# Scores of a split-precision attention: three products passed head by head, or product by product over a PSUM bank

## The chip, the cores and the metric

The kernel runs on one core of a Trainium2 chip. The metric is the device time of one execution in microseconds (us). The kernel before took 839.26 us, the median of three runs (838.55 to 841.31).

## What is computed

Three layers follow one another. The first is a linear attention with a complex decay for each of 4 batches, 8 heads, 768 positions and 48 channels of a head:

```python
new_re = ar * S_re - ai * S_im
new_im = ar * S_im + ai * S_re
kv = np.einsum('bhd,bhe->bhde', k[:, :, t], v[:, :, t])
S_re, S_im = (new_re + kv, new_im)
y[:, :, t] = np.einsum('bhd,bhde->bhe', q[:, :, t], S_re)
```

The second mixes tokens (`relu(xt @ w_tok1) @ w_tok2`, 256 wide) and channels (`relu(u @ w_ch1) @ w_ch2`, 1536 wide), each with a residual. The third mixes each token with the one before it, and gives `sigmoid(xr @ w_r) * (relu(xk @ w_k)**2 @ w_v)`.

## The kernel before, in words

The recurrence is done in chunks. A sequence of 768 positions is six chunks of 128, here called rounds 0 to 5 (`J` in the code). Within a round the scores of the 128 keys against the 128 queries are formed for each head, masked to the lower triangle, and multiplied by v; what came before the round arrives through a carried state. Every fp16 operand is a pair, a high part (`h`) and a low part (`l`), and a product of two such pairs is three matmuls that add up in PSUM: high by high, high by low and low by high. `THREE` in `attention` (line 326) lists them.

One round runs through short stages, each a function of `attention`:
- `s_b`, `s_c` (lines 523 and 547) scale q and k and turn them by the angle (`Wc`, line 549, on VectorE), and ScalarE rounds them to the high parts `qh`, `kh` (line 550).
- `s_e` (line 559) forms the low parts `ql`, `kl` on VectorE (line 562).
- `transposed` (line 519) sends each of the four through a transposing DMA on SyncE's queue into `Rc` (for odd rounds of batch 0 the k parts go to `kt`). In batch 0 the order on the queue is qh, kh, ql, kl, in the others qh, ql, kh, kl.
- `s_f` (line 568), for a group g of four heads, forms the scores of the four heads in one PSUM bank, the tile `sp`: 128 columns a head, 12 matmuls in all (each 96 rows deep, 128 columns). `MM` (line 464) issues them, so the trace shows them under line 464.
- `s_m` (line 606) masks the bank (`m`, line 608, VectorE) and rounds it (line 609, ScalarE); `s_g` (line 612) forms its low part (line 613, VectorE).
- `s_h` (line 616) forms the output `y` of the round by matmuls from q and the carried state, and from the masked scores and v; `s_u`, `s_v` (lines 580, 597) carry the state on. `s_i` (line 631) evacuates `y` to the halves `xh` and `xl`.

In batch 0 the two groups have a bank each (two buffers); in the later batches both use one bank in turn. The order in which the stages of neighbouring rounds are written stands in `ORD0` (batch 0) and `ORD1`:

```python
ORD0 = "u1 f01 f11 b0 q0 k0 e0 i2 v1 m01 m11 g01 g11 h01 h11 w0"
```

The digit at the end says how many rounds back the stage works. Within that, the framework orders the instructions of each engine when the program is built: it keeps a list by priority and planned time, takes what its plan holds ready, and keeps the instructions that write one bank in the order written. On the chip every engine then follows its list in order, whatever is ready.

Batch 0's attention runs alone, from about 50 to 121 us into the span. In its first three rounds, and in its chunk sums, matmuls that compute nothing (`keep_busy`, line 466, `h1b<-tri`) stand behind the real ones at the lowest priority. From 121 us on the dense layers of batch b (`mm3`, line 681) run with the attention of batch b+1 mixed between them, up to about 690 us; the rest is the dense work of batch 3.

Of the kernel before, what the change touches and what calls it, by code (L numbers as in the profile page):

```python
# [98 lines left out]
def split_path(  # L99
# [224 lines left out]
    def attention(b):  # L324

        THREE = (("h", "h"), ("h", "l"), ("l", "h"))
# [136 lines left out]
        def MM(**k):  # L463
            last_mm[:] = [nc.tensor.matmul(**k)]  # L464
# [103 lines left out]
        def s_f(J, g):  # L568
            d = st[J]
            sp = (ps_d if b == 0 else ps_1).tile([128, 4, 128], F32, tag="d" if b == 0 else "s", name="sp")  # L570
            with tc.high_priority(offset=P_PE):
                for i in range(4):
                    h = 4 * g + i
                    for n_, (a_, b_) in enumerate(THREE):
                        MM(out=sp[:, i], lhsT=Tr[J % 2]["k" + a_][0:96, h], rhs=Tr[J % 2]["q" + b_][0:96, h],
                                         start=n_ == 0, stop=n_ == 2)
            d["S", g] = sp
            return 0.0

# [71 lines left out]
        cq, ck = late(s_c, "q"), late(s_c, "k")  # L651
        fns = {"b": s_b, "w": s_w, "q": cq, "k": ck, "e": s_e, "i": s_i, "u": s_u, "v": s_v}
        fns.update({nm + str(g): late(fn, g) for nm, fn in (("f", s_f), ("g", s_g), ("h", s_h), ("m", s_m)) for g in range(2)})
        order = [(fns[x[:-1]], int(x[-1])) for x in (ORD0 if b == 0 else ORD1).split()]

# [527 lines left out]
```

## Time and profile before

| | |
|---|---|
| median of 3 runs | 839.26 us |
| span of the profiled execution, first to last instruction | 832.8 us |
| between the two | 6.5 us |
| TensorE matmuls (PE) busy | 747.2 us, 6287 instructions |
| VectorE (DVE) busy | 589.9 us |
| ScalarE (ACT) busy | 521.0 us |
| score matmuls (`sp`) | 576 |

The time of the profiled execution itself is not given apart from its span; the row below it sets the span against the median of the runs. PE is TensorE's matmul row, PEld its weight loads, DVE VectorE, ACT ScalarE, SPq SyncE's queue. A matmul's row includes its way through the array, so that rows overlap: how fast a run of matmuls goes is read from the time between starts. "[1.88 <-DMA Rc<-kl]" behind a row says that the engine sat idle for 1.88 us ahead of it, until the DMA from `kl` to `Rc` landed.

### The profile page before, as it was taken

The numbers are of one execution on the slowest core, as the hardware profiler recorded it, in microseconds if no ns is written. First come the engines' busy times: TensorE is split into PE (matmuls) and PEld (weight loads), VectorE is DVE, ScalarE is ACT, GpSimd is POOL, SyncE is SP. The second block draws the span as 40 slices with busy tenths as digits, with TensorE's granted clock in tenths as the row PEclk, the third lists the DMA queues.
The fourth block names the chain that finished last, engine by engine and source line by source line (L and its number), as shares of the span: only waits on it lengthen the run. The fifth ranks groups of instructions, "written<-read, shape, count | busy, mean of one in ns | idle before, by whom it ended". The sixth has DMA issues, their size and how long they took to land.

```text
span 832.8 us, 15537 instructions
## 1 busy us (share of the span) xinstructions
PE 747.2 (90%) x6287; PEld 471.7 (57%) x6287; DVE 589.9 (71%) x1028; ACT 521.0 (63%) x993; POOL 21.0 (3%) x53
## 2 busy tenths in 40 slices
PE   0977768999889789999998989999999999999996
PEld 0666645446455555665665655566665666665553
DVE  4988789999989776886857647777776534584822
ACT  7775488667659579663748787566756533142742
POOL 3000000000000000000000000000000000010000
PEclk9999979999999899999999999999999999999998
DMA  7357973356762950161525521141604432867300
GB/s 230 114 119 158 204 195 116 124 176 160 165 180 57 205 133 30 40 122 49 86 36 111 113 76 39 39 109 19 119 11 87 80 105 52 274 204 251 112 29 33
DMA packets 137950, 94.94 MB, mean 114 GB/s; under 512 B 104592, under 2 KB 120208, under 8 KB 137872
## 3 DMA queue, kind: packets, MB, share of 16 engines
q1 hardware_dynamic: 137872, 93.88, 45.0%
q8 instruction: 51, 0.84, 0.4%
q14 instruction: 27, 0.22, 0.1%
HBM read 63.97 MB, written 4.72 MB: 82 GB/s over the span
## 4 chain that ended last, share of the span: by engine, by line
PE 47%; DVE 19%; ACT 17%; DMA 12%; issue 3%; SPq 0%; ACTq 0%; DVEq 0%
PE ps L681 21%; PE a L681 14%; PE y L464 4%; DMA Rc<-kl 4%; PE sp L464 3%; ACT X L331 3%; PE u L464 2%; DVE g L774 2%; DMA X<-by_time_a_re_dram 2%; ACT tmp L812 2%; DMA Rc<-ql 2%; DVE tmp L813 1%; DVE Wc L549 1%; DMA CH<-in_qk_dram 1%; DVE wf L265 1%
## 5 line engine op out<-in xcount | busy, mean ns | idle before, releaser
L681 PEld LDWEIGHTS <-wc 128*128 128x128 f16 x1728 | 166.2, 98 | 117.2 <-issue 10.5
L681 PE MATMUL a<-g,wc 128*128 128x384 f16 x864 | 160.5, 326 | 0.0
L681 PE MATMUL ps<-uh,wc 128*128 128x384 f16 x576 | 156.1, 326 | 2.9 <-DVE g L774 1.4
L464 PEld LDWEIGHTS <-Rc 96*128 96x128 f16 (+1 forms) x1488 | 84.4, 100 | 57.8 <-DMA Rc<-kh 10.7
L681 PE MATMUL a<-wv,g 128*128 128x384 f16 x576 | 111.5, 328 | 3.3 <-ACT g L847 3.3
L681 PE MATMUL ps<-xkh,wk 128*128 128x384 f16 x384 | 105.4, 327 | 1.9 <-DVE g L848 1.9
L773 ACT ACTIVATE g<-ps 128x384 f16<-128x384 f32 x96 | 46.4, 484 | 92.8 <-PE ps L681 92.7
L681 PE MATMUL ps<-ul,wc 128*128 128x384 f16 x288 | 93.8, 326 | 0.0
L774 DVE SCALAR_TENSOR_TENSOR g<-ps,g 128x384 f16<-128x384 f32 x96 | 53.0, 553 | 45.2 <-ACT g L773 45.0
L464 PE MATMUL sp<-Rc 96*128 96x128 f16 x504 | 61.4, 229 | 26.1 <-DMA Rc<-kh 8.5
L681 PEld LDWEIGHTS <-g 128*128 128x128 f16 x576 | 54.5, 98 | 38.2 <-ACT g L847 5.2
L681 PEld LDWEIGHTS <-wk 128*128 128x128 f16 x576 | 55.0, 98 | 36.0 <-issue 4.2
L464 PE MATMUL y<-CH,Rc 96*128 96x48 f16 (+1 forms) x984 | 69.5, 188 | 6.2 <-DMA Rc<-qh 2.2
L848 DVE TENSOR_TENSOR g<-ps,g 128x384 f16<-128x384 f32 x64 | 35.4, 553 | 41.7 <-ACT g L847 41.5
L681 PE MATMUL ps<-xkl,wk 128*128 128x384 f16 x192 | 62.9, 327 | 0.0
L845 ACT ACTIVATE ps<-ps 128x384 f32<-128x384 f32 x64 | 30.3, 473 | 37.9 <-PE ps L681 33.1
L608 DVE TENSOR_TENSOR m<-sp,tri 128x512 f32<-128x512 f32 x48 | 32.6, 685 | 23.1 <-PE sp L464 23.0
L549 DVE TENSOR_TENSOR Wc<-cs,X 128x768 f32<-128x768 f32 x48 | 44.9, 950 | 0.2
L464 PE MATMUL u<-CH,kh 128*128 128x48 f16 x320 | 39.2, 185 | 2.6 <-ACT kh L550 2.6
L331 ACT ACTIVATE X<-X,col_c 128x1152 f32<-128x1152 f32 x32 | 40.1, 1252 | 0.4 <-DVE X L374 0.2
L681 PE MATMUL ps<-wr,xrh 128*128 128x384 f16 x144 | 37.8, 330 | 0.8 <-DVE g L774 0.7
L609 ACT ACTIVATE Rc<-m 128x512 f16<-128x512 f32 x42 | 26.2, 623 | 19.1 <-DVE m L608 13.5
(215 smaller groups left out, 1391.9 us busy)
## 6 DMA issues: line engine op xcount, KB each, us to landing
wst<-in_moe_w_ch_dram SPq DMA_DIRECT2D x24, 768.0 KB, 4.4
CH<-in_qk_dram SPq DMA_DIRECT2D x24, 384.0 KB, 3.3
wst<-in_moe_w_tok_dram SPq DMA_DIRECT2D x8, 768.0 KB, 4.7
wst<-in_moe_w_k_dram SPq DMA_DIRECT2D x8, 768.0 KB, 4.7
wst<-in_moe_w_v_dram SPq DMA_DIRECT2D x8, 768.0 KB, 4.5
X<-by_time_a_re_dram SPq DMA_DIRECT2D x8, 576.0 KB, 4.6
X<-by_time_a_im_dram SPq DMA_DIRECT2D x8, 576.0 KB, 5.8
CH<-by_time_v_dram SPq DMA_DIRECT2D x24, 192.0 KB, 2.9
```

What stands on the lines that cost most here:

```text
L265: STT(f, hi, -0x40000000, f, op0=ALU.bitwise_and, op1=ALU.bitwise_or)
L331: ins = ACT(out, x, fn, **k)
L464: last_mm[:] = [nc.tensor.matmul(**k)]
L549: TT(d[nm + "2"], d["cs"], bc2(hd((X3 if nm == "q" else X1)[:, J])), op=MUL)
L608: TT(m, st[J]["S", g], tri.unsqueeze(1).to_broadcast([128, 4, 128]), op=MUL)
L609: ACT(M16[g][0], m, ACTF.Copy)
L681: nc.tensor.matmul(out=ps, lhsT=lh[a_], rhs=rh[b_], start=start and n_ == 0, stop=stop and n_ == 2)
L773: ACT(part[:, 0], ps, ACTF.Relu)
L774: last_ev[:] = [STT(part[:, 1], ps, 0.0, part[:, 0], op0=MAX, op1=SUB)]
L812: ACT(w[:, 0:N], z[:, 0:N], ACTF.Copy, scale=o[:, c:c + 1])
L845: ACT(ps, ps, ACTF.Relu)
L848: last_ev[:] = [TT(part[:, 1], ps, part[:, 0], op=SUB)]
```

## The change

The two loops of `s_f` change places: all four heads of the bank pass the product (kh, qh), then all four (kh, ql), then all four (kl, qh). The flag that opens an accumulation is set at the first of the 12 matmuls alone, and the one that closes it at the last.

```diff
             with tc.high_priority(offset=P_PE):
-                for i in range(4):
-                    h = 4 * g + i
-                    for n_, (a_, b_) in enumerate(THREE):
+                for n_, (a_, b_) in enumerate(THREE):
+                    for i in range(4):
+                        h = 4 * g + i
                         MM(out=sp[:, i], lhsT=Tr[J % 2]["k" + a_][0:96, h], rhs=Tr[J % 2]["q" + b_][0:96, h],
-                                         start=n_ == 0, stop=n_ == 2)
+                                         start=n_ == 0 and i == 0, stop=n_ == 2 and i == 3)
             d["S", g] = sp
             return 0.0
```

## Rows read from the trace of the kernel before

**Rows 1.** The page: span, and the chain that ended last, by engine and line.

```profile
span 832.8 us, 15537 instructions
...
PE 47%; DVE 19%; ACT 17%; DMA 12%; issue 3%; SPq 0%; ACTq 0%; DVEq 0%
PE ps L681 21%; PE a L681 14%; PE y L464 4%; DMA Rc<-kl 4%; PE sp L464 3%; ACT X L331 3%; PE u L464 2%; DVE g L774 2%; DMA X<-by_time_a_re_dram 2%; ACT tmp L812 2%; DMA Rc<-ql 2%; DVE tmp L813 1%; DVE Wc L549 1%; DMA CH<-in_qk_dram 1%; DVE wf L265 1%
```

**Rows 2.** Stretches: length, busy us of each engine (instructions), granted clock, DMA share, GB/s.

```profile
50.00:121.00 71.00, 49.90 (x836) 42.61 (x834) 56.54 (x85) 41.40 (x74) 0.00 (x0) 0.90 0.86 184
121.00:260.00 139.00, 128.11 (x842) 72.11 (x843) 130.20 (x224) 101.46 (x189) 4.85 (x10) 0.99 0.55 150
```

**Rows 3.** TensorE's timeline, batch 0, rounds 2 to 5: start, us, instruction, idle before.

```profile
73.69 0.23 PE L464 MATMUL sp<-Rc 96*128 96x128 f16 x1 [0.56 <-DMA Rc<-kh]
...
73.98 0.22 PE L464 MATMUL sp<-Rc 96*128 96x128 f16 x1
...
75.03 0.27 PE L464 MATMUL sp<-Rc 96*128 96x128 f16 x2 [0.42 <-DMA Rc<-ql]
...
77.78 1.29 PE L464 MATMUL sp<-Rc 96*128 96x128 f16 x20 [1.88 <-DMA Rc<-kl]
...
86.47 0.80 PE L470 MATMUL h1b<-tri 128*128 128x128 f16 x6
...
89.01 1.70 PE L464 MATMUL sp<-Rc,kt 96*128 96x128 f16 x20
...
99.93 1.29 PE L464 MATMUL sp<-Rc 96*128 96x128 f16 x20 [0.77 <-DMA Rc<-kl]
...
108.82 0.37 PE L464 MATMUL sp<-Rc,kt 96*128 96x128 f16 x2 [1.05 <-DMA Rc<-ql]
...
110.02 2.31 PE L464 MATMUL sp<-Rc,kt 96*128 96x128 f16 x20
```

**Rows 4.** The chain of waits, behind the scores of round 2: start, us, what.

```profile
79.35 0.64 PE y L464 x25
...
80.50 0.83 ACT kh L550
...
81.35 5.00 DMA kt<-kh
```

**Rows 5.** VectorE's timeline around the scores of round 2.

```profile
75.34 1.81 DVE L549 TENSOR_TENSOR Wc<-cs,X 128x768 f32<-128x768 f32 x2
79.05 0.69 DVE L608 TENSOR_TENSOR m<-sp,tri 128x512 f32<-128x512 f32 x1 [1.90 <-PE sp L464]
79.66 0.95 DVE L562 TENSOR_TENSOR ql<-Wc,qh 128x768 f16<-128x768 f32 x1
```

**Rows 6.** SyncE's queue, round 1: transposes, then the load of v.

```profile
58.27 1.23 SPq L520 DMA_TRANSPOSE Rc<-qh  x1
...
62.91 1.33 SPq L520 DMA_TRANSPOSE kt<-kl  x1
64.34 0.53 SPq L514 DMA_DIRECT2D CH<-by_time_v_dram  x1
```

**Rows 7.** Waits of the scores, 120 to 690 us: total us, times, longest.

```profile
PE sp L464 <- DMA Rc<-kh: 6.6, 7, 3.2
...
PE sp L464 <- DMA Rc<-ql: 4.8, 4, 2.5
PE sp L464 <- DMA Rc<-kl: 4.7, 6, 1.5
```

**Rows 8.** TensorE's timeline, one round of batch 2.

```profile
403.18 0.28 PE L464 MATMUL sp<-Rc 96*128 96x128 f16 x2 [0.52 <-DMA Rc<-kh]
404.54 0.68 PE L464 MATMUL sp<-Rc 96*128 96x128 f16 x9 [0.47 <-DMA Rc<-kl]
```

**Rows 9.** Stretches of 10 us in batch 0, columns as in rows 2.

```profile
70.00:80.00 10.00, 6.56 (x144) 5.82 (x142) 8.10 (x14) 3.19 (x6) 0.00 (x0) 1.00 0.85 166
80.00:90.00 10.00, 7.75 (x110) 6.81 (x106) 7.74 (x12) 5.76 (x12) 0.00 (x0) 0.83 0.90 157
```

## The prediction

> **What bounds the kernel now.** I read the page's chain first: TensorE ends 47% of it, VectorE 19%, ScalarE 17%, transfers 12% [rows 1]. The scores' own matmuls are 3% of the chain, some 25 us, and the landings of kl into `Rc` 4%, some 33 us. So what stands around a late kl is worth a closer look. By stretches, batch 0's attention (50 to 121 us) has no engine that is full: PE 49.9 us of 71.0, VectorE 56.5, ScalarE 41.4, the transfers 0.86 of the time [rows 2]. It is a loop of waits. From 121 to 260 us PE (128.1 of 139.0) and VectorE (130.2) are both nearly full [rows 2]. A transfer that lands late then costs what PE idles.
>
> Next, TensorE's timeline of batch 0 [rows 3]. In round 2, when kh has landed, one score matmul of each bank runs; when ql has landed, one more of each; and 20 of the 24 run when kl has landed, after 1.88 us of idleness. That is the written order at work: within a bank, head 0's third product needs kl, and the nine matmuls of the other heads stand behind it, though six of them need only what has landed. Rounds 3, 4 and 5 show the same split of 2, 2 and 20, and so do rounds 0 and 1.
>
> Behind the 20 stands the loop itself. The mask of the first bank starts at 79.05, when 1.27 of the 1.29 us are over [rows 3, 5]. Hence the plan has the two banks take turns, matmul by matmul. Behind the burst PE runs the rest of y; ScalarE, stuck in order on y, rounds kh of the next round only at 80.50; its transpose leaves at 81.35 and lands 5.00 us later [rows 4]. On VectorE, ql of the next round stands behind the mask [rows 5]. What is taken off the burst, the next round's transposes get earlier.
>
> **The change, part by part.** No instruction is added or removed: 12 matmuls and weight loads a bank, three transposed operands awaited in the same order. What moves is which matmuls stand ahead of the wait for kl.
>
> The price of one score matmul: a burst of 20 lasts 1.29 us, of which the last row's own length is about 0.22, so starts lie 1.07/19 = 56 ns apart at granted clock 1.00 [rows 3, 9]. As the two banks take turns, successive matmuls of that burst already have different weights and different output columns. The new order therefore has no reason to go at another pace, and I price the changed neighbours at nothing. In round 3 starts lie (1.70-0.22)/19 = 78 ns apart, in round 5 (2.31-0.31)/19 = 105 ns. Of the two levels of TensorE's clock, 56 ns goes with 2.4 GHz and 105 with 1.2; 78 is a mixture.
>
> *Batch 0.* With both banks at it, 8 matmuls become ready with kh, 8 with ql, 8 with kl, in place of 2, 2, 20; so 12 fewer follow kl.
> - Rounds 2 and 4: the idle time ahead of kl is 1.88 and 0.77 us [rows 3], room for 12 x 56 ns = 0.67 us. Gain 0.67 us each.
> - Round 3: the burst follows no idle time; PE had been at its list without a pause since kh landed, but that list held filling matmuls (six in the row at 86.47, and another six after it), which are last in priority and go where the plan sees nothing else ready. I let the twelve scores take their place: 12 x 78 ns = 0.93 us. Bounds 0 (the fill stays ahead) and 0.93; nearest is the high end, because the fill is last in priority.
> - Round 5: of the twelve, six move from behind kl to behind kh, into the 1.05 us of idle time ahead of ql [rows 3]; the other six go behind ql, where PE is at work on y until the burst. So 6 x 105 ns = 0.63 us. Bounds 0 and 1.26.
> - Rounds 0 and 1: SyncE's queue is busy without a break from the transpose at 58.27 to the load of v at 64.34 [rows 6], and round 2 needs that v. The scores are not what is late. I count 0; the upper bound is 12 x 105 = 1.26 us for round 0, whose burst also ran slowly, and 0.67 for round 1.
>
> Together 0.67 + 0.93 + 0.67 + 0.63 = 2.9 us, bounds 0 and 2.9 + 0.63 + 1.26 + 0.67 = 5.5.
>
> What covers this: VectorE sat idle for 1.90 us ahead of the mask [rows 5], so 0.67 comes off idleness there and VectorE is not next. Next late is SyncE's queue with its four transposes at about 1.3 us a round [rows 6] and the transfer engines at 0.86 of the time [rows 2]; they are why the low bound is 0. The gain carries on past 121 us, since all that follows on VectorE and PE is listed behind it.
>
> *Batches 1 to 3.* One bank at a time; a late kl finds 2 of 12 matmuls done and 10 behind it [rows 8] (its second row and a single one later make the ten). With the new order up to 8 can be done, so 6 x 56 ns = 0.34 us more work stands ahead of the stall. There are six such stalls, 4.7 us in all [rows 7], nearly all longer than 0.34, so 6 x 0.34 = 2.0, less 0.2 for one of them that is only 0.17 us long: 1.8 us. The four stalls on ql (4.8 us) have 3 more matmuls ahead of them, 4 x 0.17 = 0.7 us at most; between 0 and 0.7 I count 0, as nothing else that PE could do has moved there. The seven on kh (6.6 us) are untouched. Lower bound 0: on the stretches where VectorE is full PE's idleness is not what counts.
>
> **The sum**: 2.9 + 1.8 = 4.7 us. It is worked out on an execution with a span of 832.8 us [rows 1], 6.5 below the median, and I take what lies around the span as unchanged: span 828.1, median 839.26 - 4.7 = 834.6 us. With the bounds of the parts (0 to 5.5 and 0 to 2.5) this case alone runs from 831.3 to the old time, and I give it 831.3 to 837.
>
> *Trace and rule on the clock.* The granted clock was 1.00 in the stretch with round 2's burst and 0.83 in the next [rows 9], and there starts lay 78 ns apart instead of 56 [rows 3]. PE had idled for 1.88 us ahead of the first, and the clock was full all the same. The Trainium skill, "TensorE: Matmul & The Clock Gate", section "HAM oscillation — how this bites in real kernels", advises to run all partial products of one output tile before waiting for the next transfer, as short bursts between transfers drop the clock. That speaks against this change, which spreads one bank's products over three landings. By the rows alone the sum is 834.6; by the rule it is the clock rival below.
>
> **The rivals.**
> - *The gain is hidden behind the transposes.* SyncE's queue and the transfer engines set the period of a round. For: 0.86 transfer share [rows 2], back-to-back issues in rounds 0 and 1 [rows 6]. Against: in round 2 the next kh leaves the moment ScalarE has rounded it [rows 4]. Batch 0 then gives nothing and the later batches some 1.5 us: 837.8 us. Chance 0.14.
> - *The clock drops.* In place of one long burst behind kl, three short ones between waits, and rounds that had the full clock run at round 5's pace. After kl, 8 scores at 105 instead of 56 ns cost 0.39 us more, and 25 y, 0.64/25 = 25.6 ns each [rows 4], lengthened by the same 105/56, 0.56: 0.95 us a round. In rounds 2, 3 and 4 (round 5 is slow already) 2.9 us: 834.6 + 2.9 = 837.5 us. Against it: the work of a round is the same and is spread more evenly, with shorter pauses. Chance 0.08. This is the outcome by the skill's rule just named.
> - *Slower: the masks get ahead on VectorE.* The plan now sees the scores done earlier, and so may list a round's masks and low parts ahead of the next round's `Wc`. Place: VectorE between 75.34 and 79.66 in round 2 [rows 5], and there in rounds 3 and 4. Now `Wc` ends at 77.15 and VectorE waits until 79.05. Were two masks and two low parts (four at about 0.6 us, the step from 79.05 to 79.66) listed first, from 78.38 on, `Wc` would run from 80.8 to 82.6 and kh end at 83.4 instead of 81.33: 2.1 us a round, 6.3 in three rounds. Rounds 5 (0.63) and the later batches (1.8) still give 2.4: 839.3 + 6.3 - 2.4 = 843.2 us. It decides where the planned end of the scores moves ahead of the planned start of `Wc`. Against it: in rounds 0 to 4 of the trace `Wc` of the next round is always first, in round 2 by 1.9 us to a move of 0.67. Other shifts of the plan in the later batches could cost the same way. Chance 0.16.
> - *The change doesn't do what it says.* The plan reckons all operands landed and puts other work where the scores were meant to go, so that 2, 2, 20 stays or the waits merely move. About 839.3 us. Against: 2, 2, 20 follows from the written order within a bank. Chance 0.07.
>
> **How the numbers follow.** The forecast itself keeps 0.55; its time, 834.6, is the prediction. A measurement of this kernel can tell about 0.3% (2.5 us) from no change, so faster means under 836.7 and slower over 841.8. The forecast's chance lies under 836.7 but for 0.02, and a hundredth or so of the hidden and the clock case does too: faster 0.54. Hidden, clock, no effect and that 0.02 make same 0.30. The mask case is slower: 0.16. The range from 829.5 to 843.0 leaves out half of the mask case (0.08) above, and below it about 0.05, if more rounds gain than I count. The forecast's own range is 831.3 to 837.
>
> **What would show it.** In batch 0, rows of 8, 8 and 8 scores (or split by other work) behind kh, ql and kl, the last lasting about 0.6 us in rounds 2 and 4; the mask starting 0.5 us behind kl's landing, not 1.27; rounds 2 to 5 some 0.7 us shorter each; the first dense matmuls of batch 0 about 3 us earlier; waits of the scores on kl in the later batches down from 4.7 us towards 3. The forecast is wrong if kl lands no earlier from round to round (hidden), if the granted clock between 70 and 80 us falls below 1.00 (clock), if `m` precedes `Wc` (mask), or if the gain at 121 us is given back before 690 us.

## The result, and the profile after

The changed kernel took 845.94 us (median of 6 runs, 841.25 to 846.74), the kernel before beside it 838.4 us: a ratio of 1.0078, 95% interval 1.0057 to 1.0098. It is slower by 0.8%, where a gain of 0.6% was forecast; the time lies above the range. Below, the matmuls are seen to do what the prediction said. The loss comes from instructions that the diff doesn't name.

The page of the changed kernel: span, TensorE's busy time, the chain.

```profile
span 842.4 us, 15540 instructions
...
PE 755.5 (90%) x6287; PEld 476.9 (57%) x6287; DVE 589.7 (70%) x1028; ACT 521.0 (62%) x993; POOL 21.0 (2%) x53
...
PE 46%; ACT 19%; DVE 18%; DMA 12%; issue 4%; SPq 1%; ACTq 0%; DVEq 0%
```

The shares are those of [rows 1] within two points, on 9.6 us more of span. Nothing here names a cause. TensorE's timeline of batch 0, where [rows 3] stood:

```profile
68.30 0.23 PE L464 MATMUL sp<-Rc,kt 96*128 96x128 f16 x1 [1.82 <-DMA kt<-kl]
68.37 0.19 PE L464 MATMUL y<-CH,M1l 128*128 128x48 f16 x1
...
103.46 0.62 PE L464 MATMUL sp<-Rc 96*128 96x128 f16 x8 [0.80 <-DMA Rc<-kl]
```

In round 4 eight products follow kl, not 20, and they take 0.62 us, not 1.29. Starts lie (0.62 - 0.22)/7 = 57 ns apart, as priced. But in round 1 one matmul of round 0's y, listed ahead of that wait before, now stands behind it. VectorE's timeline of batch 2, in the stretch of [rows 8]:

```profile
409.38 0.69 DVE L608 TENSOR_TENSOR m<-sp,tri 128x512 f32<-128x512 f32 x1 [1.23 <-PE sp L464]
412.42 0.96 DVE L562 TENSOR_TENSOR ql<-Wc,qh 128x768 f16<-128x768 f32 x1 [2.35 <-DMA Rc<-ql]
413.30 0.55 DVE L774 SCALAR_TENSOR_TENSOR g<-ps,g 128x384 f16<-128x384 f32 x1
413.76 0.61 DVE L638 SCALAR_TENSOR_TENSOR xl<-y,col_c,xh 128x384 f16<-128x384 f32 x1
```

The low copy of the next round's query now stands ahead of the dense evacuation `g` and of `xl`, and waits 2.35 us for a transpose of the round before, which is still reading the buffer that `ql` is to overwrite. In the kernel before, the order here was mask, `xl`, `g`, two rows of `CH`, then a low part, a mask, `kl` and only then `ql`. TensorE idles 2.23 us for that `xl`, until 414.42.

No engine got other work; the order was drawn anew. A matmul's place in the source is one input to a planner that lists every engine's instructions by estimated readiness. Compared instruction by instruction, the lists of before and after differ in 1,174 of TensorE's 6,235 matmul places, 54 of VectorE's 930, 56 of ScalarE's 919 and 3 of SyncE's 241, though the diff moves matmuls of one function only.

### The profile page after: what moved, and what is told of

It reads as the page before. It is cut to its first block, busy times and chain, and to the rows that moved or that the text cites. A ratio compares the mean times of both kernels' runs of the same rounds, so it can differ in the third digit from the quotient of the medians.

```text
span 842.4 us, 15540 instructions
## 1 busy us (share of the span) xinstructions
PE 755.5 (90%) x6287; PEld 476.9 (57%) x6287; DVE 589.7 (70%) x1028; ACT 521.0 (62%) x993; POOL 21.0 (2%) x53
## 4 chain that ended last, share of the span: by engine, by line
PE 46%; ACT 19%; DVE 18%; DMA 12%; issue 4%; SPq 1%; ACTq 0%; DVEq 0%
PE ps L681 21%; PE a L681 14%; PE y L464 4%; ACT X L331 3%; DMA Rc<-kl 3%; PE u L464 2%; PE sp L464 2%; ACT tmp L812 2%; DMA Rc<-ql 2%; DMA X<-by_time_a_re_dram 2%; DVE g L774 2%; DMA CH<-in_qk_dram 2%; DMA Rc<-kh 1%; ACT ps L845 1%; DVE tmp L813 1%
## 5 line engine op out<-in xcount | busy, mean ns | idle before, releaser
L464 PEld LDWEIGHTS <-Rc 96*128 96x128 f16 (+1 forms) x1488 | 86.6, 101 | 62.6 <-issue 16.3
L681 PE MATMUL ps<-xkh,wk 128*128 128x384 f16 x384 | 107.3, 331 | 2.3 <-DVE g L848 2.3
L464 PE MATMUL u<-CH,kh 128*128 128x48 f16 x320 | 41.9, 188 | 2.6 <-ACT kh L550 2.6
```

The source lines that it names most:

```text
L681: nc.tensor.matmul(out=ps, lhsT=lh[a_], rhs=rh[b_], start=start and n_ == 0, stop=stop and n_ == 2)
```

## The experiments

**Order and lists apart.** Theory A: the order gains as priced, the redrawn lists lose more. Rival B: the order itself costs. Rival C: neither matters. The lists can be held by dependencies that order without waiting, from each instruction of a list to the one ahead of it:

```diff
+    for lst in HELD:
+        for x, y in zip(lst, lst[1:]):
+            tc.add_manual_dep(nc.get_inst_by_name(f"I-{y}"), f"I-{x}", no_sync, reason="issue order")
...
+HELD = (
+    (
...
```

`HELD` has one list of instruction numbers for each engine, in the order wanted. The twelve products of a group trade only their own twelve places.

> New order of the scores' products, with the issue list of every engine (TensorE, VectorE, ScalarE, SyncE) held as the kernel before has it: each group's twelve products keep its twelve places in TensorE's list and only trade them among themselves, and no other instruction moves. The outputs are the reference's. Theory A (the order gains what it was priced at, and the loss comes from the lists that were drawn anew): it gains the sum of the prediction, 838.4 - 4.7 = 833.7 us (bounds 830.5 to 838.4). Theory B (the order of the products itself costs, by its pace or by TensorE's clock): it is as slow as the changed kernel, 844 to 848 us. Theory C (the products were hidden anyway, and nothing is gained or lost by their order): 838.4 us, within 0.3%, and A's half on the gain falls while its half on the lists stands.

Measured: 832.52 us, ratio 0.9918 [0.9892, 0.9944], the fastest kernel of the study. The order gains; B and C fall. In batch 0 the held places keep a part of the old split, though. TensorE's timeline of rounds 2 and 3 in this kernel:

```profile
77.41 0.83 PE L464 MATMUL sp<-Rc 96*128 96x128 f16 x12
79.91 0.62 PE L464 MATMUL sp<-Rc 96*128 96x128 f16 x8 [1.66 <-DMA Rc<-kl]
...
89.42 2.31 PE L464 MATMUL sp<-Rc,kt 96*128 96x128 f16 x20
```

In round 2 twelve products run ahead of kl. In round 3, as in rounds 0, 1 and 5, the last 20 still stand in one piece, because their places do.

The counterpart, the source of before with the lists of after:

> The counterpart: the old order, head by head, with the issue list of every engine held as the changed kernel has it. The outputs are the reference's. Theory A: the loss of the lists without the gain of the order: 845.9 us + up to 4.7 = 846 to 851 us. Theory B: the order that costs is gone, 838.4 us. Theory C: as the changed kernel, 845.9 us.

Measured: 861.74 us, ratio 1.0252 [1.0226, 1.0279]. More than A's upper end. The new lists were drawn for the new order; with the old one the products wait at places with more behind them. TensorE's idle time ahead of the scores of batches 1 to 3 in this kernel, by releaser (us, times):

```profile
  DMA Rc<-kl: 9.8, 10
  DMA Rc<-ql: 8.3, 4
  DMA Rc<-kh: 7.8, 8
```

That is 25.9 us on transposes, against 16.1 in [rows 7] with the same order of products in its own lists.

Next, new lists without a move of the waits:

```diff
+                for x_, (i, n_) in enumerate([(0, n_) for n_ in range(3)] + [(i, n_) for n_ in range(3) for i in range(1, 4)]):
...
```

> Head 0's three products first, then the other three heads product by product, so that the waits on the transposes stand at places 1, 2 and 3 of the group as before; lists left to the planner. They come out as before in all of batch 0, and in batches 1 to 3 with a part of the moves of the changed kernel (around 408 us the low copy of the next round's query is put ahead of a dense evacuation and of xl, as in the changed kernel; around 488 to 577 us a part). The outputs are the reference's. Theory A: milestones as before up to about 400 us, then +2 to +6 us: 840.5 to 844.5 us. Theory B: nine of twelve products run interleaved in all rounds, so about three quarters of the loss, in batch 0 too: 843 to 845 us with a lag of 2 to 3 us at 264 us already. Theory C (order and lists are both without effect): 838.4 us.

Measured: 842.96 us, ratio 1.0034 [1.0014, 1.0055]. The wait places are the old ones, and still it is slower, as A said. Beside the second profile of before (below) its masks are 1.5 us early at 410 us and 2.5 us late at 449, across the stretch where its lists differ. Up to 400 us, where its lists are the old ones, it is 1.5 us early beside that profile and 3.6 us late beside the first, so that stretch tells little; B fell with the held kernel.

**Which engine's list.** New order, with `HELD` cut to the lists of VectorE, ScalarE and SyncE, then to TensorE's alone (each name in brackets stands for that engine's list of numbers):

```diff
 HELD = (
-    (DVE), (Activation), (SP), (PE),
+    (DVE), (Activation), (SP),
```

> New order with the lists of VectorE, ScalarE and SyncE held as before, TensorE's list left to the planner (it places 929 of 6,235 matmuls otherwise than before, among them the last y product of round 0 behind the first score product that waits for round 1's kl). The outputs are the reference's. Theory A: the losses from 408 us on and the one of round 3 (xh ahead of the next query's copy) go; of the one in round 1 (1.4 to 2.0 us, y behind the wait on kl) the part on TensorE's list stays: 833.7 + 2 = about 836 us (833 to 840). Theory B: 844 to 848 us, as the order is the new one. If it is above the fully held kernel by over 5 us, TensorE's list alone carries most of the loss.

Measured: 839.25 us, ratio 0.9991 [0.9969, 1.0013]: 0.7% (6.7 us) over the fully held kernel, from TensorE's list alone. By what was set ahead, over 5 us, that list would carry most of the loss; the counterpart speaks against it:

```diff
 HELD = (
-    (DVE), (Activation), (SP), (PE),
+    (PE),
```

> New order with TensorE's list alone held as before; VectorE's, ScalarE's and SyncE's lists left to the planner. The outputs are the reference's. Theory A, losses that add up (the kernel with the other three held stood 6.7 us above the fully held one, the changed kernel about 6 us above that): 832.7 + 6 = about 839 us. Rival, that TensorE's list is the one that costs and the others only follow it: 833 to 835 us. Rival, that two lists that don't fit each other are worse than either: 843 us and more.

Measured: 845.24 us, ratio 1.0064 [1.0039, 1.0088]: 1.5% over the fully held kernel, above A's 839 us and in the range of the last rival. The lists of VectorE, ScalarE and SyncE come out in a third way (by the order of its rows at least 35 of VectorE's places differ from before), again with `ql` ahead, waiting 2.79 us. The two losses don't add up: 0.7 and 1.5, where the changed kernel stands 1.6% over. The rival that TensorE's list is the cost and the others follow it falls. Whether lists that don't fit each other cost more than either isn't told, as these are not the changed kernel's.

What TensorE's list does is seen around 226 us in batch 1. First the kernel before, then the fully held one, then the one with only TensorE's list redrawn (timelines of TensorE):

```profile
225.77 0.18 PE L464 MATMUL u<-CH,kl 128*128 128x48 f16 x1
228.43 0.22 PE L464 MATMUL sp<-Rc 96*128 96x128 f16 x1 [2.48 <-DMA Rc<-ql]
228.49 1.30 PE L681 MATMUL a<-g,wc 128*128 128x384 f16 x7
```

```profile
225.97 0.22 PE L464 MATMUL sp<-Rc 96*128 96x128 f16 x1
226.02 1.30 PE L681 MATMUL a<-g,wc 128*128 128x384 f16 x7
...
227.81 0.28 PE L464 MATMUL sp<-Rc 96*128 96x128 f16 x2
229.06 0.38 PE L464 MATMUL sp<-Rc 96*128 96x128 f16 x4 [0.97 <-DMA Rc<-ql]
229.84 0.40 PE L464 MATMUL sp<-Rc 96*128 96x128 f16 x4 [0.41 <-DMA Rc<-kl]
```

```profile
223.47 0.40 PE L464 MATMUL sp<-Rc 96*128 96x128 f16 x4 [0.26 <-DMA Rc<-kh]
...
229.13 0.57 PE L464 MATMUL sp<-Rc 96*128 96x128 f16 x4 [2.69 <-DMA Rc<-ql]
...
229.56 2.73 PE L681 MATMUL a<-g,wc 128*128 128x384 f16 x8
```

A group's places are spread through the list, with dense matmuls between. In the old order the second place waits for ql, and the dense matmuls behind it wait along. Held, that place has head 1's first product, which waits for nothing; eleven dense matmuls run, and the wait comes afterwards and is 0.97 us. Redrawn, all four first products are put together, the dense ones go behind the next four, and the whole wait of 2.69 us is back.

**Which batch gains.** Lists held, the new order in a part of the batches only:

```diff
+                for x_, (i, n_) in enumerate([(i, n_) for n_ in range(3) for i in range(4)] if b == 0 else [(i, n_) for i in range(4) for n_ in range(3)]):
```

> All lists held as before, the new order of products in batch 0 alone, the old one in batches 1 to 3. The outputs are the reference's. Theory A by the prediction's terms: 839.7 (the kernel before beside the last four kernels) - 2.9 = 836.8 us. Rival, that batch 0's gain is hidden and the later batches carry the 7 us: 839.7 us. Rival, that batch 0 carries all of it: 832.7 us.

Measured: 838.78 us, ratio 0.9974 [0.9954, 0.9993]: 2.2 us (0.6 to 3.9), where 2.9 were priced.

> All lists held as before, the new order in batches 1 to 3 alone. The outputs are the reference's. Theory A by the prediction's terms: 839.7 - 1.8 = 837.9 us. If batch 0's gain is hidden: 832.7 us. If batch 0 carries all of it: 839.7 us. If the gains of the two parts add up, this one's and the last one's make the 7 us of the fully held kernel.

Measured: 835.18 us, ratio 0.9949 [0.9929, 0.9968]: 4.3 us (2.7 to 6.0), where 1.8 were priced. The two add up: 0.77% against 0.82% for the whole. No run held the lists of the unchanged kernel; that the two add up speaks against a gain from holding by itself, which would stand in their sum twice. In the fully held kernel TensorE's idle time ahead of scores, 120 to 700 us (us, times), answers to [rows 7]:

```profile
  DMA Rc<-kh: 5.2, 6
  DMA Rc<-kl: 3.9, 6
  DVE m L608: 3.2, 6
  DMA Rc<-ql: 1.0, 1
```

The waits on ql went from 4.8 to 1.0 us, those on kl only from 4.7 to 3.9. This holds over more executions: with the new order and TensorE's list held in batch 1, ql's waits are 1.0, 0.6, 0.5, 0.5 and 0.3 us (the fully held kernel, this one, and three below); with the old order 4.8, 5.3 and 3.8 us (the two profiles of before, and the kernel with the new order in batch 0 alone). In the changed kernel the waits are:

```profile
PE sp L464 <- DMA Rc<-kh: 7.1, 8, 3.2
...
PE sp L464 <- DMA Rc<-ql: 4.8, 4, 2.6
PE sp L464 <- DVE m L608: 4.6, 5, 1.9
PE sp L464 <- DMA Rc<-kl: 3.4, 4, 1.9
```

kl fell as forecast, by 1.3 us; ql gave nothing, and the waits on masks rose from the 2.8 us of the kernel before to 4.6.

**How far one profile can be read.**

> The kernel before, unchanged, for a second profiled execution beside the first, which lay some 4 us under the median of its runs. No theory tells on the time: 835 to 842 us. What it is for: where in the span two executions of one program part. If they part in batch 0 and up to 300 us, by the granted clock of single stretches and with the same releasers, then the lags read against the first profile (+4.0 us at 264 us in the changed kernel) hold up to that much of chance, and only lists and releasers, not such lags, name a cause.

Measured: 839.6 us, one run; its span is 837.8, so 1.8 us lie around it, and the prediction's profile (span 832.8) was of an execution of some 834.6. The two part by 6.2 us up to one mask of batch 1 (at 265.86 and 272.03), and stay 4.0 to 5.4 us apart from 305 us on. Two stretches, columns as in [rows 2], of the first and then of the second execution, and the second one's wait:

```profile
225.00:235.00 10.00, 7.52 (x76) 4.97 (x75) 7.54 (x14) 3.94 (x8) 0.00 (x0) 1.00 0.87 179
245.00:255.00 10.00, 8.06 (x65) 4.68 (x66) 8.15 (x16) 8.59 (x20) 0.74 (x1) 1.00 0.49 83
```

```profile
225.00:235.00 10.00, 7.10 (x72) 4.39 (x71) 6.84 (x12) 4.07 (x7) 0.85 (x1) 0.83 0.91 189
245.00:255.00 10.00, 7.48 (x58) 3.92 (x55) 7.82 (x13) 7.27 (x15) 0.00 (x0) 0.78 0.72 147
```

```profile
230.42 0.27 PE L464 MATMUL sp<-Rc 96*128 96x128 f16 x1 [2.90 <-DMA Rc<-ql]
```

So the same program idles 2.48 us with the clock at 1.00 behind it, or 2.90 with 0.83, and 0.78 later, around another idle time (1.88 us in the first execution, 2.03 in the second). Of the changed kernel's lag of 4 us at 264 us against the first profile, nothing is left against the second: there its mask at 270 us is 2.0 us early. It is still 1.0 us early at 410, then 2.7 late at 452, 4.9 at 483, 7.2 at 494 and about 6 from 590 on. The loss of that execution lies in batch 2.

**Which stretch of the lists loses.** New order, lists of before, but one stretch as in the changed kernel. A difference between two of these ratios is uncertain by some 0.35%. First batch 0; on ScalarE `qh` (1223), `xh` (1232) and `kh`:

```diff
...
-1223, 1232, 1226,
+1232, 1223, 1226,
...
```

> New order, all lists held as before, but over batch 0's rounds (up to 122 us) the lists of the changed kernel: xh ahead of the next query's copy in one round, the last y product of round 0 behind the wait on round 1's low key, 564 of TensorE's places. The outputs are the reference's. The fully held kernel stood 0.8% under the kernel before. By the milestones of the profiles against the second one of before (0.85 us late at 113 us in the changed kernel, 0.67 us early in the fully held one): 1.5 us of the 13.4 us between the two, so 0.6% under before. If the delay of round 3 (6.7 us at its mask) counts in full: 2 to 4 us, 0.3 to 0.5% under. If lists cost only where all of them are drawn anew together: no difference from the fully held one, 0.8% under.

Measured: 833.3 us, ratio 0.9935 [0.9912, 0.9957], 0.17% over the fully held kernel. On ScalarE's timeline, round 3:

```profile
91.92 0.58 ACT L637 ACTIVATE xh<-y,col_c 128x384 f16<-128x384 f32 x1 [5.07 <-PE y L464]
92.40 0.83 ACT L550 ACTIVATE qh<-Wc 128x768 f16<-128x768 f32 x1
```

`xh` now stands ahead of the next query's copy and holds it for 5.07 us. It looked like a main cause, and isn't: round 3's mask is 3.9 us later than in the fully held kernel (95.54 against 91.66), round 4's two masks 0.35 and 1.3 us, round 5's not at all.

Next TensorE's 150 places in batch 1, as in the third fence above in place of the second:

> New order, all lists held as before, but TensorE's 150 places and VectorE's two of batch 1's rounds (190 to 310 us) as in the changed kernel: the wait on the low query at 229 us stands in one piece again (2.6 us; 0.97 and 0.41 us when held), and the granted clock falls to 0.83 behind it, as it does in the second profile of before, which from there is 6 us behind the first. The outputs are the reference's. Expected: 4 to 6 us of the loss, so 0.1 to 0.3% under before. If that fork is chance alone, whatever the lists: no difference from the fully held one, 0.8% under.

Measured: 834.9 us, ratio 0.9936 [0.9912, 0.9960], 0.18% over. The wait is in one piece again, 2.12 us, with the clock at 0.83 between 225 and 235 us, and all waits on ql are 3.9 us again, not 1.0: these 150 places take most of ql's gain back. This execution's mask at 269.45 is 4.0 us behind the held one's. By the medians it is 1.5 us, less than the 4 to 6 expected, and no cost at all is within the interval. What the places cost in time stays open. TensorE's wait, and the stretch as above:

```profile
229.21 0.38 PE L464 MATMUL sp<-Rc 96*128 96x128 f16 x4 [2.12 <-DMA Rc<-ql]
```

```profile
225.00:235.00 10.00, 7.88 (x74) 4.92 (x72) 6.25 (x12) 4.76 (x9) 0.85 (x1) 0.83 0.86 178
```

Batch 2, first stretch; on VectorE the mask (4817), `xl` (4704), `g` (4647), `kl` (4935) and `ql` (5237):

```diff
...
-4817, 4704, 4647, 4749, 4779, 4819, 4883, 4935, 5237, 4691,
+4817, 5237, 4647, 4704, 4749, 4779, 4819, 4883, 4935, 4691,
...
```

> New order, all lists held as before, but around 400 to 415 us as in the changed kernel: the low copy of the next round's query ahead of a dense evacuation and of xl on VectorE, the copy of that query ahead of the dense evacuation on ScalarE, 50 places of TensorE. The outputs are the reference's. By the milestones of the changed kernel between 410 and 460 us (1.0 us early to 0.8 us late, with 2.7 us between): 1.8 us, 0.6% under before; up to 3.7 us (0.35% under) if all of the peak stays. If lists cost only together: 0.8% under.

Measured: 835.89 us, ratio 0.9969 [0.9942, 0.9996], 0.51% or 4.3 us over. VectorE's timeline of this kernel, and TensorE's:

```profile
405.12 0.69 DVE L608 TENSOR_TENSOR m<-sp,tri 128x512 f32<-128x512 f32 x1 [1.30 <-PE sp L464]
408.28 0.96 DVE L562 TENSOR_TENSOR ql<-Wc,qh 128x768 f16<-128x768 f32 x1 [2.47 <-ACT CH L602]
409.15 0.55 DVE L774 SCALAR_TENSOR_TENSOR g<-ps,g 128x384 f16<-128x384 f32 x1
```

```profile
410.28 0.23 PE L464 MATMUL y<-CH,Rc 96*128 96x48 f16 x3 [2.35 <-DVE xl L638]
```

SyncE's queue, and its issues from 396 to 420 us with the median time to landing:

```profile
403.58 1.34 SPq L520 DMA_TRANSPOSE Rc<-ql  x1
```

```profile
Rc<-ql SPq DMA_TRANSPOSE x1, 4.6
```

The stall is there again with all lists outside this stretch as before, and TensorE idles 2.35 us for `xl` behind it. The releaser in `ql`'s row is only what ended last nearby: the transpose that reads `ql`'s buffer left at 403.58 and lands 4.6 us later, at about 408.2, and `ql` starts at 408.28. In the fully held kernel seven ready instructions stand between that mask and `ql`, and it starts without a wait. From the mask at 405.12 to that at 447.82 this execution falls 3.8 us further behind the held one (402.70 and 441.58).

Batch 2, second stretch, of which VectorE's first move is that of a low part (5203) and `kl` (5494):

```diff
...
-5257, 5203, 5494, 5703,
+5257, 5494, 5203, 5372,
...
```

> New order, all lists held as before, but from about 455 to 500 us as in the changed kernel, where batch 2's last rounds run beside the start of batch 3's decay: 34 places of VectorE, 44 of ScalarE, 310 of TensorE, and two transposes ahead of a load on SyncE. The outputs are the reference's. By the milestones of the changed kernel (0.8 us late at 460, 6.1 us late at 584, while the fully held one gains 0.9): 5 to 6 us, 0.1 to 0.2% under before. If lists cost only together: 0.8% under.

Measured: 835.2 us, ratio 0.9950 [0.9924, 0.9975], 0.32% over. At first sight it is the same pattern with the key:

```profile
451.86 0.96 DVE L562 TENSOR_TENSOR kl<-Wc,kh 128x768 f16<-128x768 f32 x1 [2.92 <-DMA Rc<-kl]
452.73 0.68 DVE L613 TENSOR_TENSOR Rc<-m,Rc 128x512 f16<-128x512 f32 x1
```

`kl` waits 2.92 us for the round before's transpose, with the low part of the mask, listed ahead of it in the kernel before, now behind it. But the lists of before have this wait too, 2.33 us in the kernel before and 2.29 in the fully held one:

```profile
449.27 0.96 DVE L562 TENSOR_TENSOR kl<-Wc,kh 128x768 f16<-128x768 f32 x1 [2.29 <-DMA Rc<-kl]
```

New is another stall, later in the stretch: a reduction over a tile that is still being loaded (`stat_rmin`) stands ahead of a mask that TensorE waits for. First this kernel, VectorE and TensorE, then the held one:

```profile
483.54 1.35 DVE L366 TENSOR_REDUCE stat_rmin<-X 128x1 f32<-128x1152 f32 x1 [2.02 <-DMA X<-by_time_a_re_dram]
484.81 0.68 DVE L608 TENSOR_TENSOR m<-sp,tri 128x512 f32<-128x512 f32 x1
485.54 0.44 PE L464 MATMUL sp<-Rc 96*128 96x128 f16 x5 [1.98 <-DVE m L608]
```

```profile
477.51 0.69 DVE L608 TENSOR_TENSOR m<-sp,tri 128x512 f32<-128x512 f32 x1 [1.00 <-PE sp L464]
479.35 1.35 DVE L366 TENSOR_REDUCE stat_rmin<-X 128x1 f32<-128x1152 f32 x1 [1.14 <-DMA X<-by_time_a_re_dram]
```

In the changed kernel it stands the same way, and TensorE idles 1.85 us for the mask. This execution falls 6.7 us behind the held one between the masks at 453.33 and 484.81 (452.72 and 477.51); by the medians it is 2.7 us, less than the 5 to 6 expected and within the 0.35% by which two ratios can be off. How much of it this stall makes isn't told.

Then the other way: the changed kernel's lists, with batch 2's two stretches alone as before (the last two diffs, turned round; by the lists 43 of VectorE's places, where the text below says 45).

> New order with the changed kernel's lists on all engines, except batch 2's two stretches (around 400 to 415 us and from about 455 to 500 us: 45 places of VectorE's, ScalarE's lists in all 48, 360 of TensorE's and the three of SyncE), which are as before. The outputs are the reference's. If the stretches cost here what they cost in the fully held kernel (0.51 and 0.32%, together 7 us), the changed kernel's 0.78% over before becomes 0.0% (838 to 841 us beside a before of 839.6). If the loss lies in the fit of all lists together, little changes: 844 to 846 us. If these two are all of it, whatever stands elsewhere: 0.8% under before, 832.9 us.

Measured: 836.37 us, ratio 0.9957 [0.9931, 0.9983]. From 0.8% over before to 0.4% under: the two stretches carry 1.2% (about 10 us, by 0.3% uncertain) of the 1.6% between the changed and the held kernel; one by one they made 0.8%. So batch 2's two stretches are the larger part of the loss. What stands elsewhere in the new lists takes about half of the order's gain (0.4%, by some 0.35% uncertain); in this kernel's trace the waits on ql are 4.5 us, as with the old order.

Last, lists left to the planner, with one rule in the source: from batch 1 on, the two parts of a query's copy come behind those of the key of the round before (`behind` makes its first argument follow its second in the list, without a wait):

```diff
...
+                behind([ins], last_half if nm == "q" else ())
+                last_half[:] = [ins]
...
+                    behind([ins], last_low if nm == "q" else ())
+                    last_low[:] = [ins]
```

> The changed kernel with lists left to the planner, but in batches 1 to 3 the copies of a round's query (high on ScalarE, low on VectorE) must stand behind those of the round before's key in the lists. Batch 0, batch 1 and batch 2's second stretch come out as in the changed kernel, around 400 to 415 us the low query no longer stands ahead of the dense evacuation, but places from 375 to 410 us and in batch 3 are drawn anew too. The outputs are the reference's. Theory, that one named overtaking is the cost: 0.51% less than the changed kernel, so 0.3% over before (841 to 843 us). Rival, that each new constraint moves other work and the planner's lists cost by chance as much as they gain: anything from 840 to 850 us, without the peak of +4 us between 410 and 449 us.

Measured: 839.14 us, ratio 0.9999 [0.9976, 1.0022]. The rule takes back 0.8%, more than that one stall, and comes out under both forecasts. The `ql` that stalls at 412.42 us in the changed kernel comes at 415.71 here, without a wait; the next one, at 431.32, doesn't wait either, where the changed kernel waits 3.00 us and the fully held one 3.14. The level of before is reached, not that of the held lists. How much of it is the rule and how much the other places that moved with it isn't told apart.

## Why the prediction was wrong

**The price and the split: right.** Eight, eight and eight; 57 ns a product; the mask of round 4 0.60 us behind kl's row.

**Batch 0, 2.9 us: not borne out by the traces.** The runs with everything else held gave 2.2 us (0.6 to 3.9), but the gain isn't seen where it was forecast. Starts of the first mask of a round, in the executions whose lists in batch 0 are those of before:

| | round 0 | round 1 | round 5 | from round 1 to 5 |
|---|---|---|---|---|
| old order, 3 executions, mean (range) | 61.9 (61.6 to 62.1) | 71.7 (71.4 to 72.0) | 112.3 (111.6 to 113.2) | 40.7 |
| new order, 5 executions, mean (range) | 60.9 (60.4 to 61.2) | 72.5 (71.6 to 73.6) | 112.0 (111.0 to 112.5) | 39.5 |

At the end of batch 0 the new order is 0.3 us ahead, not 2.9, and the dense matmuls don't start about 3 us earlier (at 104.7 to 105.4 us in the old order, 104.7 to 105.0 in the new). Round 0 gains 1.0 us, and round 1 loses it again, where ScalarE waits for the load of v, 0.59 us before and 2.66 in the held kernel (ScalarE's timelines of the two):

```profile
67.21 0.61 ACT L540 ACTIVATE CH<-CH,col_c 128x384 f16<-128x384 f32 x1 [0.59 <-DMA CH<-by_time_v_dram]
```

```profile
69.47 0.61 ACT L540 ACTIVATE CH<-CH,col_c 128x384 f16<-128x384 f32 x1 [2.66 <-DMA CH<-by_time_v_dram]
```

That bears out the count of 0 for these two. Rounds 2 to 5 give 1.2 us. By the prediction's own terms the held places leave only rounds 2 and 4, 2 x 0.67 = 1.3 us: what it counts for rounds 3 and 5 needs places to move, and no run tests that apart from all else that then moves. Where the 2.2 us of the medians come from is open.

**Batches 1 to 3, 1.8 us: mis-sized.** It gave 4.3 us. The term that was mis-sized is the one on ql: "between 0 and 0.7 I count 0, as nothing else that PE could do has moved there". It had: dense matmuls stood between the places of a group, and the wait moving some places down the list let eleven of them past it. In the fully held kernel the waits on ql fell by 3.8 us, those on kl by 0.8.

**The sum, 4.7 us: 6.9 us with the lists held.** The held kernel's 832.5 us lies within the range given and on the forecast's side, in part by luck: one part is smaller in the traces than forecast, the other over twice as large.

**The step that failed, and turned the sign,** stands at the opening of the parts: "What moves is which matmuls stand ahead of the wait for kl." And the one behind batch 0's sum, that the gain carries on "since all that follows on VectorE and PE is listed behind it". Both take the lists as given. They were drawn anew on four engines, and that costs 1.6%, twice the gain; batch 2's two stretches carry 1.2% of it.

**The mask rival** had the right kind and chance 0.16, and the wrong place. In batch 0 the masks didn't get ahead of `Wc`; `xh` got ahead of the next query's copy and `xl` of a mask, and that was recovered within two rounds. Its last clause, other shifts of the plan in later batches, is what happened, unpriced. Around 410 us `ql`, which must wait until the last transpose has read its buffer, got ahead of an evacuation that TensorE waits for; around 493 us a reduction that waits for a load got ahead of a mask. Why the planner's estimate put them there was not tried; that it follows from scores seen ready at other times is argued only.

**The clock rival.** Its sign did come in the changed kernel: between 70 and 80 us the granted clock is 0.84, not 1.00. But in the five executions with the new order and batch 0's lists of before it is 0.98 to 1.00 there, and 0.85 to 0.88 over 50 to 121 us, against 0.83 to 0.90 in the three with the old order. So the order alone doesn't bring it, and the rival falls. Over the whole span the held kernel has a mean granted clock of 0.981, the two profiles of before 0.978 and 0.971. By this case the rule weighed against the change (the Trainium skill, "TensorE: Matmul & The Clock Gate", section "HAM oscillation — how this bites in real kernels") doesn't decide: in the later batches spreading the products shortened TensorE's pauses instead (ql's waits, 4.8 to 1.0 us). *Hidden behind the transposes* is neither shown nor refuted: batch 0 gave 0.6 to 3.9 us by the medians, but 0.3 at its end in the traces.

**The baseline.** The sum was set against a profile of 832.8 us of span, and all of the 6.5 us to the median was taken to lie around it. 1.8 us do; the rest was that execution's own speed, most of it from the stretch between 215 and 272 us.

## What to carry to other kernels

Where a planner lists the engines, a reordering in the source is two changes: the one written, and all lists drawn anew. Hold the lists of before to measure the first alone, and compare the lists to find the second: look for an instruction that must wait (for a buffer to be read, or for a load) and now stands ahead of work that another engine waits for. And when a wait moves some places down an in-order list, count everything between the two places as cover, not only the instructions that were swapped.

## What the runs showed of the hardware

Two executions of one program part by some 5 us within 60 us: an idle time of 2.48 us left the granted clock at 1.00 (2.4 GHz), one of 2.90 us was followed by a stretch at 0.83, a mixture of that level and 1.2 GHz. In the kernel with TensorE's 150 places moved, one of only 2.12 us was followed by 0.83 too, so the length of that one idle time didn't decide it. A delay of 5 us on ScalarE in batch 0's loop, on the other hand, was gone two rounds later. A lag read at one place of one profile couldn't be taken for a cost until a kernel with that piece alone had been run.
